# Turning q of one attention group by the DMA crossbar instead of on TensorE, and reading it with a stride

## The chip, the cores and the metric

The kernel runs on one core of a Trainium2 chip. The metric is the device time of one execution in microseconds, of which the median over several runs is given. Engines are named as in the profile: PE is TensorE, DVE is VectorE, ACT is ScalarE, POOL is GpSimd, and SP is the engine whose queue issues all DMAs of this kernel. A span in the profile runs from the first to the last instruction of one profiled execution.

## The reference

Sliding-window causal attention, followed by a feed-forward layer with a squared ReLU. There are 8 batches of 8 heads, 576 tokens and head size 64. A token attends to itself and the 63 tokens before it:

```python
scores = scale * np.matmul(q, k.transpose(0, 1, 3, 2))
mask = (rel >= 0) & (rel < 64)
attn = softmax(np.where(mask, scores, -1e9))
x = np.matmul(attn, v)          # -> [8 * 576, 512], heads side by side
h = np.maximum(x @ w_in, 0.0)   # w_in  [512, 2048]
out = h * h @ w_out             # w_out [2048, 512]
```

All inputs and the output are float32; the kernel computes its matmuls in float16 with float32 sums.

## The kernel before

**Tiles and groups.** The 4608 tokens are 36 tiles of 128, and four tiles make a group of 512. Groups 0 to 6 and 8 hold the first 512 tokens of one batch each; group 7 collects the last 64 tokens of all batches. Tile i belongs to group i // 4. So tiles 8 to 11 are group 2, with which the change deals.

**The way of one group.** q, k and v are loaded as float32 and cast to float16. q and k must stand with the head dimension on the partitions for the scores, so they are turned (transposed). Scores, exponential, mask (a minimum with 0 or a large number), product with v (which carries a column of ones for the sum) and a normalisation give a tile of x. x is turned by the DMA crossbar, and the up-projection, ReLU, square and down-projection follow. Group 0 does the down-projection plainly (`O`); later groups split it into two by two blocks and need seven products (`p`) of sums of blocks of h and of w_out.

**Two ways to load and turn q and k.** Groups 0 to 2 load a whole group with one DMA of 1 MB (`load_kq`, L192): partition t takes tokens 4t to 4t + 3, so that each run in memory is 1 KB. After the cast the tile is `[partition, head pair, r, 128]`, where r is the token's place in its run. PE turns it with 16 transposes into PSUM (`turn_group`, L289), eight for each half of the head pairs, and a copy by DVE or ACT writes each half to `qT` or `kT` (`turned_group`, L297). That copy interleaves the four r, so that the columns of `qT` stand in token order. Groups from 3 on load each tile by itself in runs of 256 bytes and are turned by one crossbar DMA per group and operand (`turn_xbar`, L316).

**The order.** One text, `PROGRAM`, fixes the order on all engines. It is a list of words, each one call; each engine executes its own words in the order of the text. A word is a letter or two, numbers, and an engine after @ where there is a choice. The words used below:

- `lk`, `lq`: load k or q of a group; `dk`, `dq`, `dv`: load k, q or v of one tile. Tile loads take one of 8 buffers, which the cast frees.
- `ck`, `cq`: cast of a group's k or q; `ek`, `eq`, `cv`: of one tile's k, q or v (on POOL). `cs`, `cn`: copies of v shifted by 64 tokens.
- `Tk2.0`, `Tq2.0`: PE turns half 0 of k or q of group 2; `tk`, `tq`: the copies out of PSUM. `Kk3`, `Kq3`: the crossbar DMA on SP.
- `S9`: scores of tile 9 (16 matmuls of 64 columns, which run in pairs on the two halves of PE's rows); `SS6`: of tiles 12 and 13. `E`: exponential on ACT; `M`: mask on DVE; `V`, `VV`: product with v; `N`: normalisation on DVE.
- `xx9`: SP issues the crossbar DMA that turns x of tiles 8 and 9.
- `U5.1`: up-projection of tile 5, a quarter of the 2048 features (16 matmuls of 128 columns). It writes to one of two PSUM buffers (`ps_up`). `R` is its ReLU on ACT; `Q` its square, on ACT or, for feature quarter 2 of tiles 4 to 7, on DVE, which reads the PSUM buffer once more.
- `u2.0`: up-projection of the whole group 2, 128 features (4 matmuls of 512 columns), with `r` and `s` on ACT. It needs x of all four tiles.
- `p2.1.0`: product 1 of group 2, first half. It writes to one of two PSUM buffers, which `va` and `vc` (on DVE, some on ACT) read out. `sa`: sums of blocks of h on DVE. `z`, `vz`: stores, issued on SP.

Group 1 and parts of group 2 are handled tile by tile with `U`; from group 2 on `u` is used. PSUM tiles of transposes, scores and values share four buffers (`ps_att`). The turn of q of group 2 stands in the text after the last word of group 0's down-projection, `O0.3.3`, and before the up-projections of tiles 4 to 7. The scores read q in 64-column pieces:

```python
sc[hh][:, hp, blk, :], kT[r0:r0 + 64, hp, a0:a0 + P],
qTs["q", g][r0:r0 + 64, hp, a + 64 * blk:a + 64 * blk + 64],
```

Of the kernel before, what the change touches and what calls it, by code (L numbers as in the profile page):

```python
# [33 lines left out]
    Tq2.0 Z0.3 Tq2.1 tq2.0@D U4.0@u tq2.1@A xx7 U4.3@u R4.0 Tk2.1 Q4.0 z0.3 cv8@P R4.3 tk2.1@D  # L34
    U4.1@u dv10 Q4.3 cn8@P R4.1 U4.2@u dv11 Q4.1 cv9@P S9 R4.2 U5.2@u cn9@P E9.0 dk12 Q4.2 E9.1
    cs9@P S8 M9.0 R5.2 U5.1@u M9.1 E8.0 dk13 Q5.2 V9.0 E8.1 S10 R5.1 M8.0 U6.3@u cv10@P M8.1
    E10.0 dk14 N9.0 E10.1 V8.0 cs10@P M10.0 Q5.1 V9.1 V8.1 M10.1 cv11@P R6.3 dk15 U5.3@u N8.0
    cn10@P Q6.3 N9.1 V10.0 R5.3 cs11@P V10.1 N8.1 dq12 U5.0@u N10.0 Q5.3 ek12@P S11 N10.1 R5.0
    ek13@P xx9 U7.0@u E11.0 E11.1 M11.0 ek14@P Q5.0 M11.1 dq13 R7.0 U7.3@u Q7.0 ek15@P V11.0
    R7.3 dq14 V11.1 N11.0 U6.1@u Q7.3 N11.1 eq12@P p1.1.0 R6.1 Kk3 U6.0@u Q6.1 U7.2@u R6.0 xx11  # L40
    p1.1.1 Q6.0 eq13@P R7.2 sa1.3.0@D U6.2@u va1.0 Q7.2 dq15 eq14@P p1.2.0 R6.2 U7.1@u Q6.2 dv12
# [674 lines left out]
```

## Time and profile before

| | |
|---|---|
| median of 3 runs | 298.66 us (297.92 to 299.07) |
| the profiled execution | 298.53 us, span 296.8 us |
| PE busy | 284.6 us, 96% of the span |
| ACT, DVE, POOL busy | 220.9, 187.9, 105.9 us |
| packets of the hardware DMA queue | 159488, 59.26 MB, 89.0% of 16 engines' span |
| a transpose of q or k on PE | 96 in all, 219 ns each from start to modelled end |
| copy of half a turned group | 1225 ns on DVE, 1012 ns on ACT |
| crossbar DMA for a group's q | 6 in all, median 5.2 us from issue to landing |
| crossbar DMA for two tiles' x | 16 in all, median 3.9 us from issue to landing |

The page gives for each engine its busy time, the share of the span and the number of instructions. Matmuls are pipelined and their ends are modelled: sixteen transposes that follow each other closely take far less than sixteen times 219 ns, so the starts of neighbouring groups tell more than the durations. In the slices each digit is the busy share of one fortieth of the span in tenths. In a timeline the first two columns are the start and the length in us of a merged group of equal instructions; what stands in brackets is the idle time of the engine ahead of it and what ended it. For SP the length is the time that its queue needed for issuing, and a transfer lands later.

### The profile page before, as it was taken

How to read it: one execution, taken by the hardware profiler on the slowest of the kernel's cores; microseconds unless marked ns; L12 is line 12 of the kernel's file. 1: busy time of each engine (PE TensorE's matmuls, PEld its weight loads, DVE VectorE, ACT ScalarE, POOL GpSimd, SP SyncE). 2: the span in 40 equal slices, each digit the busy share in tenths (PEclk: the TensorE clock that was granted, in tenths of full speed). 3: DMA queues.
4: the chain of work that ended last, by engine and by line, in shares of the span. 5: the costliest groups of instructions: out<-in, count | busy, mean ns of one | idle time of the engine just before them, and what ended most of it. 6: DMA issues, size and time to landing. Idle time of an engine off the chain costs nothing.

```text
span 296.8 us, 8003 instructions
## 1 busy us (share of the span) xinstructions
PE 284.6 (96%) x3263; PEld 198.3 (67%) x3263; DVE 187.9 (63%) x397; ACT 220.9 (74%) x387; POOL 105.9 (36%) x158
## 2 busy tenths in 40 slices
PE   7879998999999989999999999999999999999994
PEld 2769954597956756765666666666666666666783
DVE  3698679959483787575846573757476396614453
ACT  2858987598878779668788778778877777876710
POOL 3434329246256522824625530614350440000000
PEclk9979999999999999999999999999999999999999
DMA  7999999999999999999999989999999805110323
GB/s 237 300 361 373 331 307 266 213 266 176 180 213 230 204 219 229 224 220 207 256 197 220 237 195 197 214 246 220 236 177 221 214 2 126 51 38 1 73 71 107
DMA packets 159525, 59.77 MB, mean 201 GB/s; under 512 B 140544, under 2 KB 154880, under 8 KB 159488
## 3 DMA queue, kind: packets, MB, share of 16 engines
q1 hardware_dynamic: 159488, 59.26, 89.0%
q8 instruction: 25, 0.41, 0.6%
q14 instruction: 12, 0.10, 0.1%
HBM read 38.80 MB, written 9.44 MB: 163 GB/s over the span
## 4 chain that ended last, share of the span: by engine, by line
PE 75%; DMA 7%; DVE 6%; ACT 5%; SPq 3%; issue 1%; POOL 0%; ACTq 0%
PE pps L583 33%; PE hps L414 32%; DMA kq_st<-in_k_dram 4%; DMA w_st<-in_moe_w_in_dram 3%; PE av L362 3%; DVE pm L351 3%; PE sc L336 3%; PE hps L405 3%; SPq L180 2%; ACT hrelu L426 2%; PE ops L467 2%; ACT h L445 2%; DVE w_sum L543 1%; PE run_ps L294 1%; DVE x_sb L373 1%
## 5 line engine op out<-in xcount | busy, mean ns | idle before, releaser
L426 ACT ACTIVATE hrelu<-hps 128x512 f32<-128x512 f32 x144 | 84.9, 598 | 42.1 <-PE hps L414 37.3
L414 PE MATMUL hps<-xT,w_in 128*128 128x512 f16 x448 | 109.2, 379 | 0.0
L445 ACT ACTIVATE h<-hrelu 128x512 f16<-128x512 f32 x132 | 83.0, 636 | 3.5
L414 PEld LDWEIGHTS <-w_in 128*128 128x128 f16 x448 | 42.6, 98 | 37.2 <-DMA xT<-x_sb 0.3
L583 PEld LDWEIGHTS <-h_sum 128*128 128x128 f16 x512 | 49.6, 98 | 15.1 <-DVE h_sum L543 0.4
L583 PE MATMUL pps<-w_sum,h_sum 128*128 128x256 f16 x384 | 48.2, 273 | 0.1
L583 PEld LDWEIGHTS <-h 128*128 128x128 f16 x384 | 36.9, 98 | 10.9 <-ACT h L445 1.1
L543 DVE TENSOR_TENSOR h_sum<-h 128x1024 f16<-128x1024 f16 x32 | 21.7, 693 | 30.0 <-PE pps L583 23.3
L345 ACT ACTIVATE pm<-sc 128x512 f16<-128x512 f32 x72 | 37.4, 610 | 3.1 <-PE sc L336 3.1
L279 POOL CAST v_ev<-st 128x512 f16<-128x512 f32 x34 | 23.3, 685 | 45.5 <-DMA st<-in_v_dram 41.9
L351 DVE TENSOR_TENSOR pm<-pm,mask_inner 128x512 f16<-128x512 f16 x56 | 31.0, 589 | 8.4 <-ACT pm L345 8.0
L583 PE MATMUL pps<-w_out,h 128*128 128x256 f16 x256 | 32.3, 273 | 0.9 <-ACT h L445 0.9
L594 DVE SCALAR_TENSOR_TENSOR ws<-pps,ws 128x512 f32<-128x512 f32 x24 | 16.5, 688 | 26.2 <-PE pps L583 26.2
L405 PE MATMUL hps<-xT,w_in 128*128 128x128 f16 x512 | 32.3, 222 | 0.1
L373 DVE TENSOR_TENSOR x_sb<-av,rden 128x256 f16<-128x256 f32 x72 | 30.6, 424 | 2.5
L601 DVE SCALAR_TENSOR_TENSOR osp<-pps,ws 128x512 f32<-128x512 f32 x32 | 21.9, 685 | 13.5 <-PE pps L583 13.5
L405 PEld LDWEIGHTS <-w_in 128*128 128x128 f16 x512 | 30.0, 99 | 0.5
L268 POOL CAST q<-st 128x512 f16<-128x512 f32 x24 | 15.8, 658 | 35.9 <-DMA st<-in_q_dram 35.9
L268 POOL CAST k<-st 128x512 f16<-128x512 f32 x28 | 18.5, 672 | 20.4 <-DMA st<-in_k_dram 20.0
L362 PEld LDWEIGHTS <-pm 128*64 128x64 f16 x576 | 11.9, 110 | 10.8 <-issue 3.8
L287 POOL COPY v_od<-v_ev 64x512 f16<-64x512 f16 x24 | 16.9, 704 | 2.5 <-ACT v_ev L279 1.1
L283 POOL COPY v_od<-v_ev 64x512 f16<-64x512 f16 x24 | 15.8, 657 | 4.7 <-ACT v_ev L279 3.5
(65 smaller groups left out, 258.6 us busy)
## 6 DMA issues: line engine op xcount, KB each, us to landing
st<-in_v_dram SPq DMA_DIRECT2D x40, 256.0 KB, 5.0
st<-in_k_dram SPq DMA_DIRECT2D x28, 256.0 KB, 4.8
out_dram<-osp SPq DMA_DIRECT2D x28, 256.0 KB, 2.7
st<-in_q_dram SPq DMA_DIRECT2D x20, 256.0 KB, 4.7
w_st<-in_moe_w_in_dram SPq DMA_DIRECT2D x4, 1024.0 KB, 12.1
w_st<-in_moe_w_out_dram SPq DMA_DIRECT2D x4, 1024.0 KB, 9.4
kq_st<-in_k_dram SPq DMA_DIRECT2D x3, 1024.0 KB, 6.6
kq_st<-in_q_dram SPq DMA_DIRECT2D x3, 1024.0 KB, 8.7
```

The costliest lines, as they stand in the source:

```text
L268: copier(e)(out=kq16(key, i // 4)[:, :, i % 4, :].rearrange("p a (b d) -> p a b d", d=D), in_=st[key, i][:].rearrange("p (a b) d -> p a b ...
L279: copier(e)(out=v_evs[slot(i)][:, :, 0:D], in_=st["v", i][:])
L345: nc.scalar.activation(out=pm[:], in_=live["s", i][hh][:], func=AF.Exp, scale=1.0 / float(D) ** 0.5)
L351: nc.vector.tensor_tensor(out=pms[i, hh][:], in0=pms[i, hh][:], in1=mask[:], op=ALU.min)
L373: nc.vector.tensor_tensor(out=xs[i // 2][:, 2 * half:2 * half + 2, i % 2, :].rearrange("p c (b d) -> p c b d", d=D), in0=av[:, :, 0:D].rea ...
L405: nc.tensor.matmul(hps[:, f, :], w_in_q[fq][:, c, f * P:(f + 1) * P], xT_of(i // 4)[:, i % 4 // 2, c, a:a + P], start=(c == 0), stop=(c == ...
L414: nc.tensor.matmul(hps[:], w_in_q[f // 4][:, c, f % 4 * P:(f % 4 + 1) * P], xT_of(g)[:, :, c, :], start=(c == 0), stop=(c == DMC - 1))
L426: nc.scalar.activation(out=hrelu[:] if key == "U" else hrelu[:].rearrange("p (f t) -> p f t", t=P), in_=hps[:], func=AF.Relu, scale=H_SCAL ...
L445: nc.scalar.activation(out=out, in_=hr, func=AF.Square)
L543: eng.tensor_tensor(out=out, in0=in0, in1=in1, op=op)
L583: nc.tensor.matmul(live["p", g, k][:, m, :], lhs, rhs, start=(f == 0), stop=(f == 7))
L601: nc.vector.scalar_tensor_tensor(out=t[:], in0=live["p", g, (2, 3, 4, 5)[c]][:], scalar=OUT_SCALE, in1=live["w", g, (0, 3, 2, 2)[c]][:], o ...
```

## The change

q of group 2 is still loaded with one DMA in runs of 1 KB and cast as before. The words `Tq2.0`, `Tq2.1` (16 transposes on PE) and `tq2.0@D`, `tq2.1@A` (one copy on DVE, one on ACT) are gone. In their place stands `Kq2`: SP issues one crossbar DMA of 512 KB between `dv9` and `xx7`. It leaves the columns of `qT` in the order r, t: token 4t + r stands in column 128 r + t. The scores of group 2 therefore read their 64 tokens as 16 places t of 4 places r each, with a step of 128 elements (256 bytes) from column to column within a run. k of group 2 stays on PE. Groups 0 and 1 are as before.

`PROGRAM` is written anew from this place to its end: apart from the five words named it holds the same words, in another order. Moved are, among others: on PE, `Tk2.1` comes first, all `U` of tile 4 follow, and `S9`, `S8`, `S10` stand behind `U5.2` and `U5.1`; on SP, `dq15` stands before `xx11`, `Kq3` two loads of v earlier, and `xx15` before `Kq4`; `p1.3.1` and `u3.8` stand between `u2.7` and `p2.1.0`; `vc1.1` stands behind the sums `sa2` and the masks of tiles 16 and 17; `SS10` stands before `p3.1.0`.

```diff
--- before.py
+++ after.py
@@ -31,80 +31,80 @@
     ta2.1@D cn6@P ta3.1@D V5.0 cs6@P V5.1 O0.2.2 N5.0 N5.1 V6.1 ck2.0@A ck2.1@P V6.0 z0.0
     ck2.2@D O0.3.0 ck2.3@A N6.1 xx5 Tk2.0 N6.0 cv7@A O0.2.3 ta4.0@D tk2.0@A cs7@P ta4.1@D z0.1
     O0.3.1 Z0.2 dv8 V7.1 O0.3.2 N7.1 cq2.0@A cq2.1@P cq2.2@D V7.0 z0.2 cq2.3@A O0.3.3 N7.0 dv9
-    Tq2.0 Z0.3 Tq2.1 tq2.0@D U4.0@u tq2.1@A xx7 U4.3@u R4.0 Tk2.1 Q4.0 z0.3 cv8@P R4.3 tk2.1@D
-    U4.1@u dv10 Q4.3 cn8@P R4.1 U4.2@u dv11 Q4.1 cv9@P S9 R4.2 U5.2@u cn9@P E9.0 dk12 Q4.2 E9.1
-    cs9@P S8 M9.0 R5.2 U5.1@u M9.1 E8.0 dk13 Q5.2 V9.0 E8.1 S10 R5.1 M8.0 U6.3@u cv10@P M8.1
-    E10.0 dk14 N9.0 E10.1 V8.0 cs10@P M10.0 Q5.1 V9.1 V8.1 M10.1 cv11@P R6.3 dk15 U5.3@u N8.0
-    cn10@P Q6.3 N9.1 V10.0 R5.3 cs11@P V10.1 N8.1 dq12 U5.0@u N10.0 Q5.3 ek12@P S11 N10.1 R5.0
-    ek13@P xx9 U7.0@u E11.0 E11.1 M11.0 ek14@P Q5.0 M11.1 dq13 R7.0 U7.3@u Q7.0 ek15@P V11.0
-    R7.3 dq14 V11.1 N11.0 U6.1@u Q7.3 N11.1 eq12@P p1.1.0 R6.1 Kk3 U6.0@u Q6.1 U7.2@u R6.0 xx11
-    p1.1.1 Q6.0 eq13@P R7.2 sa1.3.0@D U6.2@u va1.0 Q7.2 dq15 eq14@P p1.2.0 R6.2 U7.1@u Q6.2 dv12
-    p1.2.1 sa1.1.0@D R7.1 dv13 Q7.1 sa1.2.0@D sa1.1.1@D u2.0 dv14 sa1.3.1@D u2.8 r2.0 sa1.2.1@D
-    eq15@P dv15 s2.0 sa1.4.0@D p1.6.0 r2.8 sa1.4.1@D cv12@P u2.1 s2.8 Kq3 vc1.0 cn12@P u2.9 r2.1
...
-    s2.13 N14.0 N14.1 u2.14 r2.6 N15.0 Kq4 p1.3.1 s2.6 N15.1 r2.14 u2.12 sa2.1.0@D s2.14
-    sa2.3.0@D xx15 u2.7 r2.12 cv16@P sa2.2.0@D s2.12 cn16@P r2.7 vc1.1 vz1.2 s2.7 sa2.4.0@D
-    vz1.1 p2.1.0 sa2.1.1@D dv17 sa2.3.1@D p2.1.1 sa2.2.1@D SS8 dv18 va2.0 sa2.4.1@D p2.2.0 E16.0
-    dv19 E16.1 u3.8 M16.0 E17.0 M16.1 E17.1 u3.1 M17.0 dk20 r3.8 M17.1 p2.2.1 r3.1 cv17@P s3.8
...
-    s3.14 sa3.3.0@D vz2.2 cs21@P u3.15 sa3.4.0@D dv22 r3.7 cn21@P vc2.1 s3.7 r3.15 dv23 u4.0
-    sa3.3.1@D s3.15 p3.1.0 r4.0 sa3.1.1@D vz2.1 u4.8 s4.0 dk24 sa3.2.1@D SS10 r4.8 sa3.4.1@D
-    p3.1.1 s4.8 dk25 cv22@P E20.0 u4.1 E20.1 M20.0 cs22@P dk26 E21.0 p3.2.0 M20.1 E21.1 cv23@P
-    M21.0 r4.1 p3.2.1 M21.1 cn22@P dk27 va3.0 cs23@P VV10 s4.1 vc3.0 ek24@P u4.9 dq24 N20.0
...
+    Tk2.1 Z0.3 tk2.1@D U4.0@u Kq2 U4.3@u R4.0 Q4.0 cv8@P R4.3 xx7 U4.1@u Q4.3 cn8@P R4.1 U4.2@u
+    z0.3 Q4.1 cv9@P R4.2 dv10 U5.2@u cn9@P Q4.2 cs9@P R5.2 dv11 U5.1@u Q5.2 S9 R5.1 dk12 U5.3@u
+    E9.0 E9.1 S8 M9.0 Q5.1 dk13 S10 M9.1 E8.0 U6.3@u E8.1 M8.0 cv10@P E10.0 V9.0 dk14 M8.1 V9.1
+    E10.1 N9.0 cs10@P V8.0 R5.3 V8.1 M10.0 cv11@P R6.3 dk15 M10.1 Q5.3 N9.1 cn10@P V10.0 Q6.3
+    N8.0 U5.0@u cs11@P dq12 N8.1 ek12@P U7.0@u N10.0 R5.0 ek13@P xx9 S11 Q5.0 V10.1 R7.0 U7.3@u
+    N10.1 E11.0 ek14@P E11.1 dq13 p1.1.0 M11.0 R7.3 M11.1 p1.1.1 Q7.0 ek15@P dq14 Q7.3 U6.1@u
+    va1.0 eq12@P U6.0@u R6.1 Kk3 V11.0 Q6.1 V11.1 N11.0 p1.2.0 R6.0 N11.1 Q6.0 U7.2@u dq15
+    eq13@P sa1.3.0@D U6.2@u R7.2 xx11 p1.2.1 Q7.2 R6.2 eq14@P U7.1@u Q6.2 dv12 vc1.0 R7.1
+    sa1.1.0@D Q7.1 vz1.0 sa1.2.0@D dv13 eq15@P sa1.1.1@D sa1.3.1@D Kq3 sa1.2.1@D u2.0 sa1.4.0@D
+    u2.8 r2.0 sa1.4.1@D cv12@P dv14 p1.6.0 s2.0 r2.8 cn12@P u2.1 s2.8 dv15 p1.6.1 cv13@P r2.1
+    u2.9 s2.1 cs13@P dk16 va1.1 cn13@P u2.2 r2.9 dk17 SS6 s2.9 r2.2 u2.10 cv14@P E12.0 dk18
+    E12.1 p1.7.0 M12.0 cs14@P E13.0 M12.1 E13.1 cv15@P p1.7.1 dk19 M13.0 s2.2 M13.1 cn14@P SS7
...
+    p1.4.1 s2.13 r2.6 u2.14 vc1.2 s2.6 Kq4 p1.3.0 r2.14 u2.12 s2.14 u2.7 vz1.2 r2.12 dv16 p1.3.1
+    s2.12 r2.7 u3.8 sa2.1.0@D s2.7 dv17 sa2.3.0@D p2.1.0 r3.8 sa2.1.1@D dv18 p2.1.1 s3.8
+    sa2.2.0@D SS8 va2.0 sa2.2.1@D dv19 u3.1 E16.0 sa2.3.1@D E16.1 cv16@P u3.9 M16.0 dk20 E17.0
+    M16.1 E17.1 cn16@P sa2.4.0@D r3.1 SS9 cv17@P dk21 M17.0 r3.9 M17.1 s3.1 cs17@P sa2.4.1@D
+    E18.0 u3.0 dk22 cv18@P E18.1 vc1.1 E19.0 cn17@P M18.0 p2.2.0 E19.1 M18.1 cv19@P vz1.1 r3.0
+    M19.0 VV8 cs18@P s3.9 dk23 M19.1 p2.2.1 s3.0 cn18@P N16.0 N16.1 cs19@P u3.2 dq20 N17.0
+    ek20@P p2.6.0 N17.1 r3.2 ek21@P dq21 vc2.0 p2.6.1 s3.2 ek22@P u3.10 va2.1 xx17 u3.11 r3.10
...
+    cs21@P u3.7 s3.14 dv22 sa3.3.0@D cn21@P u4.0 sa3.4.0@D r3.7 dv23 vc2.1 s3.7 r4.0 u3.15
+    sa3.3.1@D vz2.1 s4.0 SS10 r3.15 dk24 u4.8 s3.15 E20.0 sa3.1.1@D u4.1 dk25 E20.1 cv22@P M20.0
+    E21.0 p3.1.0 M20.1 E21.1 cs22@P dk26 M21.0 r4.1 p3.1.1 M21.1 cv23@P r4.8 sa3.2.1@D p3.2.0
+    s4.1 cn22@P dk27 s4.8 sa3.4.1@D cs23@P p3.2.1 va3.0 ek24@P dq24 VV10 vc3.0 u4.9 N20.0 ek25@P
+    vz3.0 N20.1 u4.11 r4.9 N21.0 dq25 p3.6.0 s4.9 ek26@P N21.1 r4.11 u4.10 xx21 s4.11 ek27@P
...
@@ -153,6 +153,7 @@
     LEFT = B - 1
     SQUARE = "AAAA"
     SQUARE4 = ('ADDA', 'AADA')
+    Q_RUN = (2,)
     FQ = DFF // 4
     ident = const.tile([P, P], FP16, name="ident")
@@ -332,10 +333,14 @@
                     n = NCK + 2 * (i % 4) + blk
                     kT, a0 = kTs["k", n // 4], n % 4 * P
                 for hh in range(2):
-                    r0 = 64 * hh
+                    r0, t0 = 64 * hh, a + 64 * blk
+                    qT = qTs["q", g][r0:r0 + 64, hp, :]
+                    if g in Q_RUN:
+                        qT = qT.rearrange("d (r p) -> d p r", p=P)[:, t0 // 4:t0 // 4 + 16, :]
+                    else:
+                        qT = qT[:, t0:t0 + 64]
                     nc.tensor.matmul(
-                        sc[hh][:, hp, blk, :], kT[r0:r0 + 64, hp, a0:a0 + P],
-                        qTs["q", g][r0:r0 + 64, hp, a + 64 * blk:a + 64 * blk + 64],
+                        sc[hh][:, hp, blk, :], kT[r0:r0 + 64, hp, a0:a0 + P], qT,
                         start=True, stop=True)
         live["s", i] = sc
```

## The prediction

> **What bounds the kernel now.** I read the page first (busy shares, the slices), then the timelines of PE, ACT, DVE and the DMA-issuing queue SP around the edit, then the waits, then single transfers by tile.
>
> ```profile
> PE 284.6 (96%) x3263; PEld 198.3 (67%) x3263; DVE 187.9 (63%) x397; ACT 220.9 (74%) x387; POOL 105.9 (36%) x158
> DMA  7999999999999999999999989999999805110323
> q1 hardware_dynamic: 159488, 59.26, 89.0%
> ```
>
> PE is busy 96% of the span; the transfers fill the 16 engines 89% of it, at 9 in nearly every slice to about 232 us. So two resources run without slack, and the last 60 us belong to PE alone.
>
> Laying the plan's words over the PE records gives each word's start. Usual pitches: an `U` (16 matmuls) 0.89 us, `u` or `p` 0.87, an `S` 0.24 of its own. Beyond these pitches PE loses only 3.7 us in all after 58.3; five places hold most of it: 0.67 and 0.52 between `V` words near 68.5 and 70.5, 0.26 before `u2.1`, 0.87 to 1.05 inside `p2.1.0`, 0.57 in `VV10`. The last three make 1.9. That, with the removed work, is all an edit can win.
>
> The place of the edit, PE and then ACT and DVE:
>
> ```profile
> 58.33 1.06 PE L294 MATMUL run_ps<-ident,q 128*128 128x128 f16 x16
> 59.23 1.95 PE L405 MATMUL hps<-xT,w_in 128*128 128x128 f16 x32
> 63.34 0.41 PE L336 MATMUL sc<-qT,kT 64*128 64x64 f16 x16
> 65.16 1.05 PE L405 MATMUL hps<-xT,w_in 128*128 128x128 f16 x16
> ...
> 59.43 1.01 ACT L300 COPY qT<-run_ps 128x1024 f16<-128x1024 f16 x1 [0.25 <-PE run_ps L294]
> 60.34 0.60 ACT L426 ACTIVATE hrelu<-hps 128x512 f32<-128x512 f32 x1
> ...
> 58.98 1.23 DVE L300 COPY qT<-run_ps 128x1024 f16<-128x1024 f16 x1 [0.37 <-PE run_ps L294]
> 64.41 0.69 DVE L447 SCALAR_TENSOR_TENSOR h<-hps,hrelu 128x512 f16<-128x512 f32 x1 [1.53 <-ACT hrelu L426]
> ```
>
> The 16 turns take 58.33 to 59.23: 0.90. `U5.1` at 65.16 starts as the square `Q4.2` (64.41 to 65.10) frees its PSUM buffer.
>
> The SP queue, and the one wait of PE's weight load for a DMA after the start-up:
>
> ```profile
> 58.76 0.42 SPq L180 DMA_DIRECT2D st<-in_v_dram  x1
> 59.27 2.42 SPq L394 DMA_TRANSPOSE xT<-x_sb  x1
> 61.79 0.53 SPq L482 DMA_DIRECT2D out_dram<-osb  x1
> 62.37 1.18 SPq L180 DMA_DIRECT2D st<-in_v_dram  x2
> 63.65 5.26 SPq L180 DMA_DIRECT2D st<-in_k_dram  x4
> 69.01 0.82 SPq L180 DMA_DIRECT2D st<-in_q_dram  x1
> 71.72 1.23 SPq L394 DMA_TRANSPOSE xT<-x_sb  x1
> ...
> 78.79 1.90 SPq L394 DMA_TRANSPOSE xT<-x_sb  x1
> ...
> 82.70 1.19 PEld L414 LDWEIGHTS <-w_in 128*128 128x128 f16 x7 [0.27 <-DMA xT<-x_sb]
> ```
>
> The transpose issued at 78.79 (`xx11`) lands 3.87 later, at 82.66; the first wide up-projection of group 2, `u2.0`, starts at 82.70. Here the DMA stream has no slack. Between 69.83 and 71.72 SP pauses 1.9 us, waiting for `x_sb`: the only gap over 0.6 from 59 to 146.
>
> [...] the six `qT` transposes take 3.05 to 4.03 us of SP (median 3.27) and land 4.4 to 6.1 us after issue. [...] No matmul in this trace reads its moving operand with a long step, so that is open.
>
> **The change part by part.** *Removed:* 16 turns on PE (0.90), a DVE copy (1.225), an ACT copy (1.012). But `U4.0` reads the transpose `xx5`, issued at 54.16 and landing 4.77 later, at 58.93. PE can start it no sooner than about 58.97 instead of 59.23: 0.26 of the 0.90 comes out. ACT's first relu moves from 60.34 to about 60.05.
>
> *Moved on PE.* Scores of tile 9 now follow `U5.2` and `U5.1`. Relu and square on ACT repeat every 1.17 us (60.34, 61.51, 62.66, 63.80), slower than PE's 0.89, and ps_up has two buffers. So `R4.2` is at about 63.56, `Q4.2` ends at 64.85, `U5.1` starts at 64.9: 0.25 earlier than before, while `S9` and `S8` (0.34 each with their switch) are not done yet. `S9` comes at about 65.9 instead of 63.34, the exponentials 2.3 later; behind them queue masks, values and norms. At `V10.0` (69.93 before) both plans have done the same PE words except the turns; I get 71.2 by following buffers, E and M: 1.3 behind. The old 0.52 wait at `V10.1` then goes, and a little of the strided read comes on top: PE would reach `u2.0` near 83.6.
>
> *Strided scores.* 64 matmuls of 64 columns in 32 pairs, 0.24 us for a tile's 8 pairs. A step of 256 bytes at each column: lower bound no cost (columns and count are the same, so a gain is excluded), upper bound my choice of fourfold, +2.9 in all (4 x 0.24 x 3). I take twofold, +0.9, and count it in the walk above.
>
> *Added:* `Kq2` on SP, between `dv9` and `xx7`, from about 59.3. It needs the four casts, done by 58.1, so it does not wait itself; 3.27 us of SP, landing near 64.5, before `S9`. Queued behind it: `xx7`, a store, `dv10`, `dv11`, `dk12` to `dk15`, `dq12`, `xx9`, each up to 3.3 later. POOL's casts wait for these loads, and `Kk3` waits for the last of those casts. The 1.9 pause absorbs part, but `N8.1`, which `xx9` needs, is itself later with the scores: `xx9` at 72.9 (+1.2). `Kk3` needs the cast of `dk15`: about 76.5 against 75.12 (+1.4). `dq15` (0.57) is now ahead of `xx11`: 80.8 against 78.79, +2.0; landing 3.9 to 4.5 later, about 84.9. So `u2.0` starts about 2.2 late; PE's own 83.6 lies under that wait, and so do the strided reads. Bounds: +1.0 (PE's own lag alone, if the DMA engines take `Kq2` in the 1.8 us by which earlier such transposes delay the next landing) and +3.3 (nothing absorbed).
>
> *Moved later in the plan.* Same PE work from here on. `p1.3.1` and `u3.8` now stand between `u2.7` and `p2.1.0`: its wait goes; those of `u2.1` and `VV10` (its masks now precede two sums) as well: -1.9. Against that `vc1.1`, which frees the PSUM buffer of `p2.2.0`, moves behind five sums and four masks: counted along DVE it ends up to 1.1 after PE wants it; I take +0.7 (bounds 0 and 1.1). `SS10` moves ahead of `p3.1.0` and `u4.8`, 1.7 earlier, while its `Kq5` landed at 139.76 for a start at 140.97 and will land with the stream's lag: +0.8 (bounds 0 and 1.5). Other reorderings (stores, loads within a group, sums of the last groups) I put at nothing: PE's order from `p6.3` on is unchanged, and PE's steady stream hides them.
>
> *Sum:* +2.2 - 1.9 + 0.7 + 0.8 = +1.8 on the profile's span of 296.8. That execution took 298.53 by the device time against a median of 298.66 (297.92 to 299.07), so the span's difference carries over: 300.5, rounded to 300.4.
>
> **The rivals.** A difference under 0.5% (1.5 us) is about what a measurement of this kernel cannot tell from none.
>
> *It evens out.* `Kq2` costs the stream only its 1.8 us of landing time, `u2.0` is 1.2 late, and the repaired waits return that with 0.7 of new ones: 1.2 - 1.9 + 0.7 = 0: about 298.7. For it: the landings of `Kq4` and `Kq5` come only 1.7 to 1.8 after the one before. Against: `Kk3` came 3.3 after its forerunner, and the scores are late without any DMA.
>
> *Faster.* SP's pause swallows `Kq2`, ACT and DVE use their freed 1.0 and 1.2 to bring the scores of group 2 forward, and `xx11` lands in time. It decides at `u2.0`: if that starts by 82.0, the gain of 0.7 there plus 1.9 of repaired waits gives 296.1; with half of the new waits 296.8. For it: ACT is full from 58.6 to 71 and loses a copy. Against: the `xx5` landing and the `Q4.2` buffer hold PE back whether the turns are there or not.
>
> *Slower by far.* The strided read costs fourfold and the pairs no longer overlap: beyond the 1.3 that `u2.0`'s wait hides, +1.3 to +2: about 302.
>
> **How the numbers follow.** Slower 0.46 (0.36 the forecast, 0.10 the far case), evens out 0.35, faster 0.19. The forecast's own range is 299.6 to 301.6. To leave out no more than 2 in 10 the range goes from 297.0 (half of the faster case) to 302.3.
>
> **What the changed profile would show.** Right: a transpose of q on SP near 59.3, `xx11` issued near 80.8, PE's wait for xT before the first 512-wide up-projection near 2 us instead of 0.27, that step at 84 to 85.5; the 0.87 wait near 110 gone; a gap before `p2.2.0`. The pitch of group 2's scores (0.24 a tile before) shows the stride: 0.45 is my value. Wrong: no wait for xT there and `u2.0` before 82.7, or scores at an unchanged pitch together with `S9` near 64.

## The result and the profile after

The changed kernel takes 302.88 us (median of 4 runs, 302.27 to 303.03) against 298.87 (4 runs, 297.92 to 299.30): a ratio of 1.0135, 95% interval 1.0106 to 1.0164. It is 4.0 us slower. The forecast was slower, at 300.4; the time lies above its range, which ended at 302.3. The profiled span grew from 296.8 to 301.3 us.

The page after, with the same three lines as before:

```profile
PE 286.4 (95%) x3247; PEld 199.8 (66%) x3247; DVE 188.6 (63%) x396; ACT 220.0 (73%) x386; POOL 106.3 (35%) x158
DMA  7999999998999999899999999999999925110323
q1 hardware_dynamic: 161568, 59.78, 90.1%
```

Sixteen PE instructions are gone, but PE is busy 1.8 us longer. The timeline of PE after, at the place of the edit and at the start of group 2's wide up-projection:

```profile
58.20 0.61 PE L295 MATMUL run_ps<-ident,k 128*128 128x128 f16 x8
58.65 5.09 PE L410 MATMUL hps<-xT,w_in 128*128 128x128 f16 x80
64.56 1.05 PE L410 MATMUL hps<-xT,w_in 128*128 128x128 f16 x16 [0.82 <-DVE h L452]
65.54 1.05 PE L342 MATMUL sc<-qT,kT 64*128 64x64 f16 x16
66.53 1.07 PE L410 MATMUL hps<-xT,w_in 128*128 128x128 f16 x16
...
86.50 1.90 PE L419 MATMUL hps<-xT,w_in 128*128 128x512 f16 x8 [1.00 <-DMA xT<-x_sb]
88.24 0.60 PE L588 MATMUL pps<-w_sum,h_sum 128*128 128x256 f16 x4
89.73 0.61 PE L588 MATMUL pps<-w_sum,h_sum 128*128 128x256 f16 x4 [0.89 <-DVE h_sum L548]
```

`U5.1` starts at 64.56, `S9` at 65.54. `S9` and the next `U` stand 0.99 apart: a tile's 16 score matmuls took 0.34 from start to next start before, so each tile of group 2 costs 0.65 more, four tiles 2.6. `u2.0` starts at 86.50 after 1.00 us of waiting for xT. A wait for a sum of h follows inside `p1.6.0`, ahead of `u2.1`. The kernel before had 0.26 there, and its two steps were:

```profile
82.70 1.90 PE L414 MATMUL hps<-xT,w_in 128*128 128x512 f16 x8
84.44 1.29 PE L583 MATMUL pps<-w_sum,h_sum 128*128 128x256 f16 x8
```

SP after:

```profile
58.91 3.26 SPq L320 DMA_TRANSPOSE qT<-q  x1
...
65.42 5.26 SPq L181 DMA_DIRECT2D st<-in_k_dram  x4
70.78 0.80 SPq L181 DMA_DIRECT2D st<-in_q_dram  x1
74.30 2.55 SPq L399 DMA_TRANSPOSE xT<-x_sb  x1
...
78.21 3.47 SPq L320 DMA_TRANSPOSE kT<-k  x1
81.73 0.57 SPq L181 DMA_DIRECT2D st<-in_q_dram  x1
82.44 1.89 SPq L399 DMA_TRANSPOSE xT<-x_sb  x1
```

`Kq2` takes 3.26 us and all behind it moves, but SP's pause ahead of `xx9` did not shrink: it grew from 1.89 us to 2.72 (71.58 to 74.30). `xx9` waits for the normalisation `N8.1`, and that is late. DVE after, the last normalisation of tile 8 and those of tile 11, which `xx9` and `xx11` need, and then the last one of tile 11 before:

```profile
73.81 0.42 DVE L378 TENSOR_TENSOR x_sb<-av,rden 128x256 f16<-128x256 f32 x1
...
80.88 0.18 DVE L377 RECIPROCAL rden<-av 128x4 f32<-128x4 f32 x1 [3.47 <-PE av L367]
...
81.64 0.42 DVE L378 TENSOR_TENSOR x_sb<-av,rden 128x256 f16<-128x256 f32 x1
```
```profile
75.33 0.42 DVE L373 TENSOR_TENSOR x_sb<-av,rden 128x256 f16<-128x256 f32 x1
```

`N8.1` ends at 74.23, 0.07 before `xx9`. `N11.1` ends at 82.06, 6.3 later than before (75.75): it is 0.4 from being the last release of `xx11` itself, where before it had 3 us of slack. DVE had been idle for 3.47 us, waiting for `V11`.

Laying the program's words over the records of both traces, aligned at the start of `O0.3.3`, gives where the time is lost: `V10.0` +2.1, `U7.3` +3.0, `u2.0` +3.9, `u2.1` +4.7, the last product +4.6. All of it is lost before 91 us.

The wait for xT at `u2.0` does not decide this. In a second profile of the changed kernel (e13 below) it is 0.35 instead of 1.00, but the wait in `p1.6.0` is longer by as much:

```profile
85.41 1.90 PE L419 MATMUL hps<-xT,w_in 128*128 128x512 f16 x8 [0.35 <-DMA xT<-x_sb]
89.26 0.61 PE L588 MATMUL pps<-w_sum,h_sum 128*128 128x256 f16 x4 [1.51 <-DVE h_sum L548]
```

`u2.0` is then at +3.3, and `u2.1` again at +4.7. In both profiles PE itself, with the last word ahead of `u2.0` done, is ready 2.9 later than in the kernel before (85.47 against 82.55, aligned). DVE's sums need the squares of that late work, and `p1.6.0` needs the sums.

### The profile page after: what moved, and what is told of

Same layout as the page of the kernel before. It is cut to its first block, busy times and chain, and to the rows that moved or that the text cites. A ratio compares the mean times of both kernels' runs of the same rounds, so it can differ in the third digit from the quotient of the medians.

```text
span 301.3 us, 7967 instructions
## 1 busy us (share of the span) xinstructions
PE 286.4 (95%) x3247; PEld 199.8 (66%) x3247; DVE 188.6 (63%) x396; ACT 220.0 (73%) x386; POOL 106.3 (35%) x158
## 4 chain that ended last, share of the span: by engine, by line
PE 69%; DMA 12%; DVE 5%; SPq 5%; ACT 4%; POOL 3%; issue 1%; POOLq 0%; DVEq 0%; ACTq 0%
PE pps L588 29%; PE hps L419 28%; DMA kq_st<-in_k_dram 4%; PE sc L342 4%; PE hps L410 3%; DMA w_st<-in_moe_w_in_dram 3%; PE av L367 3%; SPq L181 3%; PE ops L472 2%; DVE pm L356 2%; DMA st<-in_v_dram 2%; ACT hrelu L431 2%; DMA qT<-q 2%; DMA st<-in_q_dram 1%; DVE h_sum L548 1%
## 5 line engine op out<-in xcount | busy, mean ns | idle before, releaser
L588 PE MATMUL pps<-w_sum,h_sum 128*128 128x256 f16 x384 | 47.0, 273 | 1.1 <-DVE h_sum L548 0.9
L548 DVE TENSOR_TENSOR h_sum<-h 128x1024 f16<-128x1024 f16 x32 | 22.9, 730 | 30.4 <-PE pps L588 22.9
L356 DVE TENSOR_TENSOR pm<-pm,mask_inner 128x512 f16<-128x512 f16 x56 | 32.0, 604 | 10.1 <-ACT pm L350 9.5
L588 PE MATMUL pps<-w_out,h 128*128 128x256 f16 x256 | 31.1, 273 | 0.0
L284 POOL COPY v_od<-v_ev 64x512 f16<-64x512 f16 x24 | 16.9, 703 | 5.3 <-ACT v_ev L280 4.2
L288 POOL COPY v_od<-v_ev 64x512 f16<-64x512 f16 x24 | 16.7, 697 | 2.5 <-ACT v_ev L280 1.1
```

Source lines behind the costliest of these rows:

```text
L356: nc.vector.tensor_tensor(out=pms[i, hh][:], in0=pms[i, hh][:], in1=mask[:], op=ALU.min)
L548: eng.tensor_tensor(out=out, in0=in0, in1=in1, op=op)
L588: nc.tensor.matmul(live["p", g, k][:, m, :], lhs, rhs, start=(f == 0), stop=(f == 7))
```

## The experiments

Seventeen runs of thirteen builds, the changed kernel among them. In the table "new" is the order of words after the edit, "strided" the read with 256 bytes from column to column. The last three columns are starts of words in the profiled execution against the kernel before, aligned as above; "dip" marks a profile in which PE's granted clock falls to 0.50 for 3.41 us between `O0.3.3` and the last column.

| run | order | q turned by | read | ratio (95% interval) | u2.0 | u2.1 | last p |
|---|---|---|---|---|---|---|---|
| e2 | old | PE | strided | 1.0053 (1.0032 to 1.0074) | +0.9 | +1.5 | +1.1 |
| e3 | old | crossbar | plain | 1.0039 (1.0018 to 1.0060) | +1.8 | +1.5 | +1.1 |
| e5 | old | crossbar | strided | 1.0102 (1.0063 to 1.0142) | +3.0 | +3.8 | +3.7 dip |
| e4 | new | PE | plain | 1.0094 (1.0072 to 1.0117) | +1.9 | +3.0 | +2.7 |
| e16 | new | PE | plain | 1.0151 (1.0126 to 1.0177) | +2.7 | +3.2 | +2.6 |
| e15 | new | PE | strided | 1.0207 (1.0182 to 1.0231) | +3.5 | +5.4 | +4.8 |
| e1 | new | crossbar | plain | 1.0104 (1.0074 to 1.0135) | +2.9 | +4.8 | +4.5 dip |
| e14 | new | crossbar | plain | 1.0149 (1.0124 to 1.0173) | +3.3 | +4.0 | +3.7 dip |
| after | new | crossbar | strided | 1.0135 (1.0106 to 1.0164) | +3.9 | +4.7 | +4.6 |
| e13 | new | crossbar | strided | 1.0142 (1.0119 to 1.0164) | +3.3 | +4.7 | +4.6 |
| e17 | new | crossbar | plain | one execution, 302.57 us | +3.3 | +4.7 | +4.4 dip |
| e9 | new, sums earlier | crossbar | strided | 1.0147 (1.0118 to 1.0177) | +3.4 | +4.1 | +3.4 |
| e12 | old to `U7.3`, then new | PE | plain | 1.0039 (1.0020 to 1.0058) | +0.1 | +1.3 | +1.1 |
| e6 | old to `u2.0`, then new | PE | plain | 1.0021 (1.0004 to 1.0039) | -0.5 | +0.1 | +0.8 |

e4 and e16 are one build on two chips, and their intervals do not meet; e1 and e14, again one build, differ nearly as much. The granted clock explains part of it. Most profiles (13 of the 18 other than e7's), that of the kernel before included, have a dip to 0.50 for some 3.4 us near 20 us; one such dip is 0.006 of an execution's mean clock (3.4 x 0.5 / 300). Of e4's six executions four have a mean clock of 0.999 or 1.000, of e16's none (0.988 to 0.994), while six of the eleven of the kernel before beside e16 are at 1.000. At 1.000 alone the kernel before takes 296.5 to 298.2 on five chips, e4 300.3 to 300.9 and the changed kernel, once, 302.5. The word starts are aligned after the early dip and are free of it. So small differences are read below between runs of one chip or from word starts.

### The parts in the old order

*e2: the strided read alone.* The read and `Q_RUN` are put into the kernel before; everything else is as it was.

```diff
+    Q_RUN = (2,)
...
+                    qT = qTs["q", g][r0:r0 + 64, hp, :]
+                    if g in Q_RUN:
+                        qT = qT.rearrange("d (r p) -> d p r", p=P)[:, t0 // 4:t0 // 4 + 16, :]
...
```

> The kernel before with its order and its turn on PE; only the scores of group 2 read with the step of 256 bytes, so that they meet other tokens of q and batch 2 is not the reference's. STRIDE theory: PE is packed here, so all four steps show, 4 x 0.65 = 2.6 us, and the wait at u2.0 does not hide it: 300.9 to 302. DMA theory: the stride is hidden behind waits, under 0.8 us: 298.9 to 299.7. ORDER theory: 1 to 2.6 us, since it says only that the order adds its own share.

299.80 us, +0.53%: less than STRIDE had and within what ORDER allowed. Each score step grows by the same 0.65 as after the change. Of the 2.6 us so added some 1.1 to 1.6 remain; `V10.0` already comes only 1.1 later after three of the four tiles, so the rest seems to have gone into waits that PE had there anyway.

*e3: the crossbar alone.* The old order, with `Kq2` in the place of the turns.

```diff
-    Tq2.0 Z0.3 Tq2.1 tq2.0@D U4.0@u tq2.1@A xx7
+    Z0.3 U4.0@u Kq2 xx7
```

> The order of the kernel before with Kq2 in the place of the two turns and two copies of q (between dv9 and xx7), read with neighbouring columns, so batch 2 is not the reference's. DMA theory: xx11 and u2.0 come 2 to 3 us later, 300.8 to 302. STRIDE theory: SP's pause of 1.9 us before xx9 takes most of the transfer and 0.26 to 0.9 us of PE are saved: 298 to 299.6. ORDER theory: like the stride theory, with a wait of up to 0.8 at S9, which stands earlier here: 298.5 to 299.5.

299.50 us, +0.39%, where DMA had 300.8 to 302. PE of this build, the scores of tile 9 and `u2.0`, and the last steps of its SP queue:

```profile
65.29 0.41 PE L336 MATMUL sc<-qT,kT 64*128 64x64 f16 x16 [1.71 <-DMA qT<-q]
85.14 1.90 PE L414 MATMUL hps<-xT,w_in 128*128 128x512 f16 x8 [1.62 <-DMA xT<-x_sb]
```
```profile
72.98 3.19 SPq L394 DMA_TRANSPOSE xT<-x_sb  x1
...
77.52 4.28 SPq L319 DMA_TRANSPOSE kT<-k  x1
81.90 1.26 SPq L394 DMA_TRANSPOSE xT<-x_sb  x1
```

Here the forecast's mechanism is seen by itself: `xx11` goes out at 81.90 instead of 78.79 (2.5 later when aligned) and PE waits 1.62 for its landing. `S9` waits 1.71 for q besides; in the new order `S9` comes later, and that wait is gone.

*e5: crossbar and stride in the old order*, e3 with the read of e2 (so the whole change except the order).

> The order of the kernel before with Kq2 in the place of the PE turn and the strided read: everything of the change but the new order, and computing the reference. If the order is the main cost (it alone cost 2.8 us, the crossbar alone 1.2, the stride alone 1.6): 1.5 to 2.8 us over before, thus well under the change's 4.0; the stride partly hides in the wait for xx11 that the crossbar makes. If the stride and the crossbar make the change slow whatever the order: 3.5 us or more over before.

301.83 us. The ratio, +1.0% or 3.0 us, is about the sum of e2 and e3, lies between the two ranges that were expected, and has a wide spread. Of the twelve executions the four with a mean granted clock of 0.997 to 0.998 took 299.4 to 299.7, the other eight, at 0.983 to 0.989, 301.2 to 304.1 (the profile is one of those, with a dip at 66.8 to 70.2). At 0.997 to 0.998 the kernel before took 297.1 to 298.2 beside it, so without a second dip the change in the old order costs some 2 us.

*e7 and e11: the queue position.* e3 with `xx11` moved ahead of `Kk3`. The profiled execution of e7 had a mean granted clock of 0.657 and took 412 us, so the word starts come from e11, one more execution of the same build.

```diff
-    eq12@P p1.1.0 R6.1 Kk3 U6.0@u Q6.1 U7.2@u R6.0 xx11
+    eq12@P p1.1.0 R6.1 xx11 Kk3 U6.0@u Q6.1 U7.2@u R6.0
```

> The kernel of e3 (order of before, Kq2, neighbouring columns, which are other tokens for batch 2) with one word moved: xx11 is issued on SP ahead of Kk3 instead of behind it. QUEUE theory (u2.0 waited 1.8 us in e3 because Kq2 pushes xx11 behind in one queue, and Kk3 has time): the wait at u2.0 goes and the time is 0.8 to 1.6 us under e3, at most 0.3 over before. LANDING theory (the 16 engines are full, so that xx11 lands late wherever it is issued): the wait stays over 1 us.

> One more profile of e7 (crossbar in the old order, xx11 ahead of Kk3), whose own profile ran at a clock of 0.657 and can't be compared. QUEUE theory: u2.0 waits under 0.3 us for the transpose of x. LANDING theory: over 1 us. As e7's time stayed that of e3, a third reading is that u2.0 is in time and another wait takes what it gave, such as S9's wait for Kq2 and p1.6.0's for a sum.

e7: 299.67 us, +0.39% (0.22 to 0.57), the same as e3, and neither QUEUE nor LANDING. In e11 `xx11` goes out at 77.29, and `u2.0` has no wait for xT:

```profile
82.62 1.90 PE L414 MATMUL hps<-xT,w_in 128*128 128x512 f16 x8
```

It starts 0.25 behind the kernel before, but this execution took 301.52, and the word starts drift from +0.15 at `u2.1` to +3.5 at `VV8`: +1.9 at `SS8` through waits at `SS6` and `SS8`, the rest around a clock dip at 112.8 to 116.3. So the queue position cures the place where the wait is seen, and the median of e7 says that nothing is won by it in the end; which later wait takes it back is not settled by one execution with a dip in it.

### The order

*e4 and e16: the order alone.* The changed kernel with the turns of q put back on PE and the plain read.

```diff
-    Tk2.1 Z0.3 tk2.1@D U4.0@u Kq2 U4.3@u
+    Tq2.0 Z0.3 Tq2.1 tq2.0@D Tk2.1 tq2.1@A tk2.1@D U4.0@u U4.3@u
-    Q_RUN = (2,)
+    Q_RUN = ()
```

> The new order with q of group 2 turned on PE as before (Tq2.0 and Tq2.1 ahead of Tk2.1, copies on DVE and ACT), no Kq2, neighbouring columns, which are the right tokens here. ORDER theory: the scores are late for PE's buffers and u2.0 with them, 301 to 302. STRIDE theory: the order alone costs 1 us before u2.0 and wins 1 to 1.9 after it: 298 to 299.5. DMA theory: without the transfer xx11 is back in time, 297.5 to 298.9.

> The new order alone, turns on PE, q read contiguously, beside the run before on one chip. Both theories: 0.9% above the kernel before, 300.5 to 301.2; no clock dip in the profile.

300.74 and 302.29 us: +0.9% and +1.5%, on two chips. e4 lies near ORDER's 301 to 302; e16 missed its range of 300.5 to 301.2. With no crossbar transpose and no stride more than half of the loss is there, +2.6 to +2.7 at the last product. SP of e4, and DVE's normalisations of tile 11:

```profile
72.51 1.24 SPq L399 DMA_TRANSPOSE xT<-x_sb  x1
...
75.15 3.44 SPq L320 DMA_TRANSPOSE kT<-k  x1
78.64 0.57 SPq L181 DMA_DIRECT2D st<-in_q_dram  x1
79.66 1.70 SPq L399 DMA_TRANSPOSE xT<-x_sb  x1
```
```profile
78.44 0.18 DVE L377 RECIPROCAL rden<-av 128x4 f32<-128x4 f32 x1 [3.09 <-PE av L367]
79.21 0.42 DVE L378 TENSOR_TENSOR x_sb<-av,rden 128x256 f16<-128x256 f32 x1
```

SP is free again at 79.21, but `xx11` goes out at 79.66, as `N11.1` ends at 79.63. The new order puts `p1.1.0`, `p1.1.1`, `U6.1` and `U6.0`, four steps of PE or 3.5 us, between `U7.3` and `V11.0`. And `xx9` at 72.51 follows `N8.1`, which is late because the scores stand behind `U5.1`.

*e12 and e6: which part of the order.* e12 keeps the old order up to `U7.3`, e6 up to `u2.0`, both with the turns on PE; from there on the words follow in the new order (in e6 `vc1.0` and its store keep their old place behind the sums).

> The order alone (q turned on PE, read in token order), with the old order until U7.3 and the new one from there. The kernel with the new order throughout was 1.0094 of before, the one with the old order until u2.0 1.0021. SCORES theory (the scores behind U5.2 and U5.1 cost 1.3 us by U7.3): 1.004 to 1.006. SUMS theory (the block from p1.1.0 to u2.1, with V11 late and U7.1 last, costs the most): 1.007 to 1.009.

> q turned on PE, read in token order, the order of the kernel before until u2.0, and from there that of the changed kernel (vc1.0 and its store vz1.0 stay behind the sums sa1). EARLY theory (the new order loses its time between U4.0 and u2.1): no loss here, and the waits repaired at p2.1.0 and VV10 against the new ones at u3.0, p2.2.1, p2.7.0: within 0.7 us of before. LATE theory (the new order after u2.0 costs): 2 us or more over before, like the order alone.

e12: 299.02 us, +0.39% (0.20 to 0.58), at the edge of SCORES. e6: 298.82 us, +0.21% (0.04 to 0.39), which is EARLY. Taken from e4's 0.94%, the words up to `U7.3` cost 0.55%, about 1.6 us, those from there to `u2.0` 0.5 us and the rest 0.6. All three are differences between chips, but the word starts at the last product (+2.7, +1.1, +0.8) give nearly the same: 1.6, 0.3 and 0.8.

e12 also bears on `V11.0`, which stands there behind the same four steps as in e4 and starts 3.1 late. `N11.1` is again the last release of `xx11` (it ends at 78.64, and `xx11` goes out at 78.67), but `u2.0` is only 0.05 late. So the move of `V11.0` by itself costs nothing at `u2.0`; most of the order's cost comes with the words up to `U7.3`, where the scores stand behind `U5.2` and `U5.1`.

*e9: the sums.* In the changed kernel `p1.2.1` stands behind `U7.1`, and the read-out `vc1.0` behind the sums `sa1`, so that DVE reaches the sum sooner for which `p1.6.0` waits.

```diff
-    R7.2 xx11 p1.2.1 Q7.2 R6.2 eq14@P U7.1@u Q6.2 dv12 vc1.0 R7.1
+    R7.2 xx11 Q7.2 R6.2 eq14@P U7.1@u p1.2.1 Q6.2 dv12 R7.1
...
-    u2.8 r2.0 sa1.4.1@D cv12@P dv14 p1.6.0
+    u2.8 r2.0 sa1.4.1@D vc1.0 cv12@P dv14 p1.6.0
```

> The changed kernel, stride and all, with two words moved: U7.1 stands ahead of p1.2.1 on PE, and vc1.0 (with its store) behind the sums sa1 on DVE. SUMS theory (the 1.07 us wait inside p1.6.0 is for the sum sa1.2.1, which the new order made late): that wait goes and u2.0 stays where it was, 0.8 to 1.1 us less than the changed kernel, 1.0095 to 1.011 of before. If p1.6.0 only passes on the delay of something else, the wait turns up again within the next ten words and the time stays at 1.0125 or more.

302.57 us, 1.0147 (1.0118 to 1.0177): by the times, taken on another chip than those of the changed kernel, there is no gain. The profile is ahead of the changed kernel's by 0.7 at `u2.1` and by 1.2 at the last product, about as much as SUMS expected, though the wait in `p1.6.0` falls only from 0.89 to 0.71 and `U7.1` now waits 0.52 for a square. Whether the sums are worth that much is left open; most of the loss, +3.4 at the last product, is there without them.

*e10: the repairs in the old order.* In the kernel before `p1.3.1` stands between `u2.7` and `p2.1.0`, and the masks of tiles 20 and 21 ahead of two sums: the waits that the forecast had expected to win.

> The kernel before, q of group 2 turned on PE, with two repairs that the new order showed: p1.3.1 stands behind u2.7, so that p2.1.0 does not wait for the last square, and the masks of tiles 20 and 21 stand ahead of the sums sa3.2.1 and sa3.4.1. If the 1.05 and 0.57 us of PE's waits there are the path to the end: 1.2 to 1.6 us under before, ratio 0.9946 to 0.996. If another wait takes their place: within 0.5 us of before.

298.37 us, 1.0009 (0.9993 to 1.0025). Its profile is 0.67 ahead at the last product, which the times do not show. No build here beats the kernel before.

### The strided read

*e8: a ladder of steps.* The kernel before, with another spacing of the columns for each tile of groups 2 and 3 (the matmuls read other tokens of q).

```diff
+    STEP = {8: 2, 9: 4, 10: 8}
+    RUN = {11: 16, 12: 2, 13: 4, 14: 8}
...
+                        qT = qT.rearrange("d (p s) -> d p s", s=STEP[i])[:, 0:64, 0]
...
+                        qT = qT.rearrange("d (c x) -> d c x", x=8 * n)[:, :, 0:n]
+                    elif i == 15:
+                        qT = qT.rearrange("d (r p) -> d p r", p=P)[:, 16 * blk:16 * blk + 16, :]
...
```

> The kernel before with the scores of tiles 8 to 15 reading q at other columns, so batches 2 and 3 are not the reference's; the count of matmuls is the same. Tiles 8, 9, 10: a step of 4, 8, 16 bytes; 11, 12, 13, 14: runs of 16, 2, 4, 8 neighbouring columns; 15: the change's step of 256 bytes. LINE theory (each access to a new 16-byte line costs): 0.24 us a tile at 4 bytes, dearer as fewer columns share a line, 0.9 at 16 bytes and at 256 bytes alike; runs of 8 and 16 near 0.24, runs of 2 about half of 0.9. STEP theory (any step that isn't one element costs the same): 0.9 at 4 bytes already.

The scores of tiles 9, 8, 10 and 11 in PE's timeline (8, 4 and 16 bytes from column to column, and runs of 16 columns):

```profile
62.55 0.64 PE L348 MATMUL sc<-qT,kT 64*128 64x64 f16 x16
64.12 0.41 PE L348 MATMUL sc<-qT,kT 64*128 64x64 f16 x16
65.71 1.09 PE L348 MATMUL sc<-qT,kT 64*128 64x64 f16 x16
70.68 0.41 PE L348 MATMUL sc<-qT,kT 64*128 64x64 f16 x16
```

From start to start a pair of matmuls takes 31 ns at 4 bytes, 57 at 8, 113 at 16 and 109 at 256; in runs of 16 or 8 columns 31, of 4 columns 32, of 2 columns 57; plain 30.5. With four fp16 columns in 16 bytes the read is free (31 and 32 ns), with two it runs at half speed (57), with one at about a quarter (113), and 256 bytes (109) are no worse than 16. That is LINE, with the runs of 2 at 57 ns. The 16 bytes follow from these rows: counted by 8 bytes, steps of 4 bytes and runs of 2 would both have two columns, but they take 31 and 57 ns; counted by 32 bytes, steps of 8 bytes and runs of 4 would both have four, but they take 57 and 32.

*e1, e14 and e17: the changed kernel with the plain read* (`Q_RUN = ()`; q is still loaded in runs of 1 KB in all three), *beside e13, the changed kernel again.*

> The changed kernel with its crossbar turn and its new order, but the scores of group 2 read 64 neighbouring columns of qT, not columns 256 bytes apart. Those columns hold other tokens of q, so the scores of batch 2 are not the reference's; amount and kind of work are. STRIDE theory (each score step of group 2 costs 0.65 us more on PE, which makes the norms of tile 8, the transpose of x and u2.0 late): the four steps fall from 0.9 to 0.24 us and about 3 us of the 4.0 come back, 299.5 to 300.3. DMA theory (the crossbar transfer pushes the full queue): under 1 us comes back, 302 to 302.9. ORDER theory (scores placed behind U5.2 and U5.1): about 1 us back, 301.5 to 302.

> The changed kernel as it is, to stand beside the next run on one chip. All theories: 1.3% above the kernel before, 302.0 to 303.0 us.

> The changed kernel with q of group 2 loaded without the 1 KB runs, so that the scores read it contiguously (other tokens of q stand in the columns; the output differs for that). STRIDE theory (in the new order 2.6 us of score steps in front of u2.0 still cost about 1 us at the end): 301.3 us, 0.9 to 1.7 below the run beside it, and in the profile score tiles with a pitch of 30 ns and u2.0 about 1 us earlier. Rival, ORDER theory (the new order and the crossbar already leave the idle time in which the longer score steps lie): within 0.4 us of the run beside it, with the score steps' time turned into waits at u2.0, u2.1 and the value steps.

> A third profile of the changed kernel with q of group 2 read contiguously. CLOCK theory (PE's denser work after U4.0 brings the clock down in every execution of this build): granted clock 0.50 for about 3 us near 71 to 75, as in the two profiles before. CHANCE theory (the dips belonged to those executions): 1.00 throughout.

301.01 us in e1, but 302.40 in e14 beside 302.68 for e13 on the same chip: in e14 the 2.6 us of longer score steps are worth nothing by the times, as ORDER had expected. But the reason that the traces suggest is another one, PE's clock. Here are windows of the trace (columns: engines' busy time, PE's granted clock, DMA share, GB/s), first e14, then the changed kernel of the first result:

```profile
68.00:72.00 4.00, 2.49 (x55) 2.00 (x53) 3.90 (x10) 3.36 (x7) 2.89 (x5) 0.94 0.95 200
72.00:76.00 4.00, 4.00 (x62) 3.71 (x61) 1.66 (x7) 2.43 (x5) 2.41 (x5) 0.63 1.23 163
```
```profile
68.00:72.00 4.00, 3.21 (x78) 2.78 (x72) 2.49 (x7) 3.62 (x8) 2.54 (x4) 1.00 0.90 188
72.00:76.00 4.00, 3.47 (x65) 2.96 (x64) 2.65 (x9) 2.55 (x6) 3.89 (x7) 1.00 0.82 161
```

With the plain read the clock is halved for some 3.4 us from 71.5, while PE has work. The two `U` that fall into it, in e14:

```profile
71.32 3.44 PE L410 MATMUL hps<-xT,w_in 128*128 128x128 f16 x32
```

32 such matmuls took 1.95 us in the kernel before, so 1.5 us are lost. All three profiles of this build have such a second dip, though not at one place: e1 from 71.2, e14 from 71.5, e17 from 85.8, where CLOCK had expected it near 71 and CHANCE none. The three profiles with order, crossbar and stride (after, e13, e9) have none between 23 us and the end. In the timed executions too the plain build has the lower mean clocks: 0.987 to 0.992 in e14, 0.994 to 1.000 in e13.

What goes ahead of a dip can be counted in the traces. In each profile the clock changes only on a grid of 3.413 us (in the kernel before it is 1.00 for 4 such stretches, 0.50 for one and 1.00 for 81), and the grid lies differently in each execution (that dip starts at 18.16 us, the changed kernel's at 18.63). For every stretch at full clock one adds up the columns of moving operands that PE takes in. A pair of score or value matmuls, which run together, counts once, and a matmul that crosses an edge counts by its share, at the 0.43 ns a column of the `U` steps. Rounded to tens: between 8 us and the end the 18 profiles other than e7's have 1501 such stretches, half of them with more than 7700 columns. All 28 with at most 2890 are followed by a dip; none of the 1473 with at least 2990 is. Ahead of the second dips stand 1610 columns (e1), 1840 (e14), 1040 (e17), 2150 (e5) and 2860 (e11). In e17 that is the stretch in which `u2.0` waits for xT:

```profile
85.64 3.48 PE L419 MATMUL hps<-xT,w_in 128*128 128x512 f16 x8 [2.80 <-DMA xT<-x_sb]
```

So in these traces a wait of PE that leaves so little work in a stretch is paid twice (in e17 2.80 us of waiting, then 3.4 us at 0.50), and the plain read is the more exposed: wherever 3.413 us are laid on the trace between 58 and 95 us, the changed kernel takes in at least 3150 columns (after, e13, e9 alike) and the kernel before 3750, while the three traces of the plain build go down to 1500, 1810 and 890. This is a count without an exception, not an experiment in which the columns alone were varied.

*e15: the stride in the new order, where no dip masks it.* e16 with `Q_RUN = (2,)`, on one chip with e16.

> The new order with the turns still on PE (as in e4_order_alone), and the scores of group 2 read with the 256-byte step (the copies write q contiguously, so other tokens are read; the output differs for that). No crossbar transpose. STRIDE theory (the step costs its own 0.65 us a tile, hidden in the contiguous build by a granted clock of 0.50 for 3 us near 72): 302.0 to 302.8, 1.2 to 2.0 above the run beside it, neither with a clock dip. ORDER theory (the longer steps lie in idle time that the new order has anyway): within 0.5 of the run beside it, 300.5 to 301.2.

304.05 us against 302.29: 1.8 us more, or 1.0207 against 1.0151. That is the difference of STRIDE, though both times lie above their ranges. Three of e16's six executions have a mean clock of 0.988 to 0.989 and none of e15's; at 0.992 to 0.994 alone the medians are 301.89 and 304.07, 2.2 apart. In the profiles, both without a second dip, the last product comes 2.2 later as well. The scores of tiles 9 and of 8 with 10, first e15, then e16:

```profile
65.57 1.05 PE L342 MATMUL sc<-qT,kT 64*128 64x64 f16 x16
67.55 1.94 PE L342 MATMUL sc<-qT,kT 64*128 64x64 f16 x32
```
```profile
66.81 0.41 PE L342 MATMUL sc<-qT,kT 64*128 64x64 f16 x16
68.15 0.78 PE L342 MATMUL sc<-qT,kT 64*128 64x64 f16 x32
```

And e15 at `u2.0` and in `p1.6.0`:

```profile
85.18 1.89 PE L419 MATMUL hps<-xT,w_in 128*128 128x512 f16 x8
89.54 0.61 PE L588 MATMUL pps<-w_sum,h_sum 128*128 128x256 f16 x4 [2.02 <-DVE h_sum L548]
```

Here PE does not wait for xT at all, and `u2.1` is later than in any other build, at +5.4: PE's own lateness is what is carried on.

So the stride costs 2 us of its 2.6 in the new order. By word starts the sum closes: the order +2.6, the stride +2.2, and the crossbar in the place of the turns -0.1 (e15's +4.8 to +4.6 with the crossbar). The times of e15, at 1.0207 on another chip, lie above the 1.0135 and 1.0142 of the changed kernel; by them the crossbar would win up to 2 us, and which of the two holds is open. With the crossbar the plain read should take some 2 us out, and the dip puts 1.5 back in. In e17, which is at full clock up to `u2.0`, PE is ready for `u2.0` at 83.02 (aligned), 2.4 before the changed kernel, but then waits for xT. That this is why e14 equals e13 is worked out, not shown: no profile of the plain build is free of a second dip. Its one execution at 0.999 (in e1) took 299.9; those of the changed kernel at 0.999 and 1.000 (in e13) took 302.0 and 302.5.

## Why the forecast was wrong in size

The direction was right, and so was the place: everything is lost ahead of `u2.1`. The step that failed is the first term of the sum, "+2.2" at `u2.0`, and in it the sentence that PE's own 83.6 and the strided reads lie under the wait for `xx11`. `u2.0` came to +3.9 (+3.3 in the second profile). PE's own arrival came to 85.47, 1.9 later than 83.6, and it is this arrival that reaches the end: `u2.1` is at +4.7 with 1.00 us of waiting for xT (after), with 0.35 (e13), and at +5.4 with none (e15). That the direction came out right is in part luck, since `Kq2`, to which the forecast gave much of the +2.2, adds nothing in the new order by word starts. Point by point:

- *Strided scores.* Mis-sized: twofold was taken (+0.9), the read is 3.6-fold (109 ns a pair against 30.5, +2.6). The upper bound had it at fourfold, +2.9; the middle was chosen without a row behind it. Of the 0.9 only "a little" went into the 83.6; PE's arrival in e17 (plain read) and in the changed kernel lies 2.4 apart. Nor could the reads lie under the wait for `xx11`: they make PE late itself, and scores also delay masks, values and `N8.1`, these delay `xx9`, and with it `Kk3` and `xx11`. In e16 and e15 `xx9` goes out 2.0 and 3.4 after its place in the kernel before, `xx11` 2.1 and 4.2.
- *The order on PE.* `V10.0` was put at +1.3 before the stride. The builds with the plain read and no turns (e1, e14, e17) show +1.2, +0.9 and +0.7, those with the turns (e4, e16) +1.5 and +1.8. Right, or a little high. Overlooked was that `V11.0` had moved behind four steps of PE: `N11.1`, which had 3 us of slack, is the last release of `xx11` in e4, e13, e15 and e16. By e12 that alone costs nothing at `u2.0`.
- *Kq2 on SP.* Its issue (3.26 for 3.27), its landing (64.15 for 64.5) and `S9` unharmed by it were right. In the old order it makes `xx11` 2.5 late and `u2.0` 1.8 (e3). But in the new order it adds nothing: `xx11` goes out +4.2 without `Kq2` (e15) and +3.8 with it. `xx11` near 80.8 and `u2.0` at +2.2 were thus nearly what e4 shows without any `Kq2` (80.55 and +1.9): the number had the wrong owner.
- *The pause of SP* was to absorb part of `Kq2`. It grew to 2.72, since what ends it is `N8.1`.
- *The removed turns.* `U4.0` was forecast at 58.97 and `U5.1` at 64.9; they came at 58.65 and 64.56 (58.78 and 64.69 aligned). The numbers are near, the reason was not: `xx5` had landed at 58.09, and `U4.0` follows `Tk2.1` at once. Against e15, which has the same order and read with the turns on PE, the whole 0.90 is out at `U4.0` and `S9`, 0.7 of it at `u2.1`, and 0.1 at the last product.
- *u2.1.* Its wait of 0.26 was to go, for which the forecast gave no reason. It became 1.07 in `p1.6.0` (1.5 in e13), for a sum on DVE that waits for PE's late work. e9, with the sums moved, has 0.7 less at `u2.1` by its profile and nothing by its times.
- *Later waits.* Gone as forecast: the waits of `p2.1.0` and `VV10`, 1.6 together. The +0.7 at `p2.2.0` did not come, and the +0.8 at `SS10` came to 0.23. In their place stand 0.74 inside `VV8`, 0.33 at `p2.7.0` and 0.22 at `u3.0`, 1.5 together with `SS10`. From `u2.1` to the end the net is -0.1, as in the forecast; that the sum is right is luck, since its parts are not.

The profile's +4.6 exceeds the sum of +1.8 by 2.8, and all of it is there at `u2.1`. How it divides between `u2.0` and `u2.1` differs from profile to profile (1.7 and 1.1 after, 1.1 and 1.7 in e13). e15 beside e16 gives the stride 2.2 at `u2.1`, for which the forecast, having it under the wait, had next to nothing; the remaining 0.6 is not assigned. The rival "slower by far" had named the stride, with a chance of 0.10 and a time of about 302; its pairs that no longer overlap are not seen (the two of a pair still start 3 to 4 ns apart). The sum itself holds, but for a slip in its last step: 298.66 and 1.8 make 300.5, not 300.4.

## What to carry to other kernels

A price that no row of the profile shows should keep its upper bound in the forecast until something speaks for less, and a cost is hidden under a wait only if the engine that pays it still arrives before the wait ends and the cost does not feed what that wait is for: follow both through. A wait that ends last in one profile may be short in the next of the same build, so check on a second profile that it is what reaches the end. When an order is rewritten, list for each late transfer all of its releases and how far each has moved, not only the one that was last before. And when a part is removed and nothing is gained, look at the granted clock before concluding that the part was free.

## What was not expected of the hardware

- In e8 PE read an fp16 moving operand of 64 columns at nearly the plain pace (31 to 32 ns for a pair against 30.5) as long as four columns shared 16 bytes; it took 57 ns with two, 113 with one, and 109 at 256 bytes.
- The granted clock fell to 0.50 for 3.4 us in the middle of a busy kernel, in three of three profiles of one build and in none of three of its neighbour: 1.5 us in e14, nearly as large as the effect that was studied. In 18 profiles it followed every stretch of 3.41 us in which PE took in at most 2890 columns, and none with 2990 or more. The dips near 20 us, which come and go from execution to execution of one build, follow the same count.
- One build on two chips gave 1.0094 and 1.0151, with intervals of about 0.0025 to either side.
